# A gated linear-attention and SiLU feed-forward kernel: the state's product in two column tiles, the second product of the feed-forward without Strassen's method

## The chip, the cores and the metric

The kernel runs on one core of a Trainium2 chip. The metric is the device time of one execution in microseconds; shorter is better. Engines are named as in the profile: PE is TensorE (PEld its weight loads), DVE is VectorE, ACT is ScalarE, POOL is GpSimd, and SP is SyncE, which here only issues DMAs.

## What is computed

The inputs are `q`, `k`, `v`, `a_re`, `a_im` of shape (4, 8, 768, 48) and two weight matrices of 384 x 2048 and 2048 x 384 (the reference makes them in 64 bits; the kernel puts them together to 32 bits at the start). Cut to what matters:

```python
mag = np.sqrt(a_re * a_re + a_im * a_im)
scale = np.minimum(mag, 0.999) / (mag + 1e-06)
a = a_re * scale + 1j * a_im * scale          # per head and channel
for t in range(768):
    S = a[t][:, None] * S + outer(k[t], v[t]) # complex state, 48 x 48 per head
    y[t] = q[t] @ S.real
x = y with heads side by side                 # (3072, 384)
h = x @ w_in                                  # (3072, 2048)
out = (h * sigmoid(h)) @ w_out                # (3072, 384)
```

## The kernel before

**Tiles.** The 4 sequences of 768 steps are cut into chunks of 128 steps: 24 chunks, numbered n = 0 to 23, so that chunk n follows chunk n - 4 of the same sequence. Two chunks make a pair p = 0 to 11. The complex gates become, by logarithms and phases, a factor per step, so that a chunk's attention is plain products: `weights` (L410) makes 128 x 128 products of keys and queries for each of 8 heads, masked by DVE (L415); `output` (L431, L434) multiplies them with `v`, and adds the part from the state `S` carried from chunk n - 4; `state` (L459) makes the chunk's own part of the next state, and DVE adds and scales it (L464, L465, or L467 for a sequence's first chunk). The last chunk of each sequence makes no state, so that 20 states are made.

**The state's product.** For each of 8 heads the 128 x 96 keys (`kr`, real and imaginary part side by side) are TensorE's weights and the 128 x 48 values its moving operand; the result stands on 96 partitions of one PSUM bank. A 32-bit product is two load-and-multiply pairs on TensorE, so that the profile counts 16 for one state. `output` works in two tiles of 64 of TensorE's columns: even heads write partitions 0 to 63, odd heads 64 and up.

**Feed-forward.** A pair's 256 rows of `x` go through `hidden` (L476: eight steps of 12 matmul records of 128 x 256, each step followed by a SiLU on ACT, L245) and `result`. `result` for pairs 0 to 2 is the plain one (L518): per step two row halves times two blocks of `w_out`, 8 records of 128 x 384, in two PSUM banks. From pair 3 (`WINO = 3`, nine pairs) it is `result_of_halves` (L545): Strassen's method on halves of rows, of the inner dimension and of columns, seven products of 128 x 192 per step, 14 records. It needs four sums per step by DVE (`sums_of`, L505), combined weights made once (L493, L496), three products with zeros that open the PSUM banks (L539, per pair), and at the end of a pair an ACT copy (L552) and seven DVE additions (L556).

**What sets the order.** In the set-up (pairs 0 to 2) PE's order is written out, and a scheduler orders the other engines. From pair 3 on `step` is called under a manual schedule: all engines follow the program's order, and the strings `first` and `usual` give it token by token. In a step, `h` is a step of `hidden` and `r` one of `result`, both for the pair before; `a0A`, `a1A`, `sA`, `yA` are weights (two halves), state and output of the pair's first chunk, with B for the second; `k`, `q`, `t` rotate and turn keys and queries; `p` and `l` are the products for phases (L325) and sums (L346) of the next pair; E, D, L, F, G, th are the gates on ACT and DVE; A and X load the next inputs. ACT loads a table of functions (L240) when it changes between exponentials, arctangent and SiLU.

**Queues.** From chunk 8 on `turned` moves 12 blocks of transposed keys and queries by DMA (L401), six issued by SP and six by POOL. `output` moves six small pieces of `xT` at the end of a pair (L448), three from SP and three from POOL. SP also issues the loads, POOL the decays (`decs`, L360), ACT the stores (L529).

Of the kernel before, what the change touches and what calls it, by code (L numbers as in the profile page):

```python
# [55 lines left out]
def kernel(  # L56
# [36 lines left out]
    EARLY = 8  # L93
    RAW = 4
    WINO = 3
# [127 lines left out]
    zeros = consts.tile([1, DM], mybir.dt.bfloat16)  # L223
    nc.gpsimd.memset(zeros, 0.0)
# [30 lines left out]
    def gates_square(p, split=False):  # L255

        g = A[p]
        for x in ("s1", "s2", "mag"):
            g[x] = flat(pre.tile([C, 2, H, D], F32, tag="t3", name=f"{x}{p}", bufs=5))
        for x in ("l", "th"):  # L260
            pool = su if p == 1 else pre
            g[x] = flat(pool.tile([C, 2, H, D], F32, tag=x, name=f"{x}{p}"))
        for re, im, s1, s2, _, _, th in each(p, split):
            special(s1, re, AF.Square)
            special(s2, im, AF.Square)
            special(th, re, AF.Abs)
            nc.vector.scalar_tensor_tensor(out=s1, in0=s1, scalar=FLOOR2, in1=s2, op0=ALU.max,
                                           op1=ALU.add)
# [50 lines left out]
    def phases(n):  # L319
# [4 lines left out]
        ps = p_m.tile([C, DM], F32, tag="m", name=f"phase{n}")  # L324
# [9 lines left out]
    def trig(n):  # L334
        x = X[n]
        x["cs"] = pre.tile([C, H, 2, D], F32, tag="t3", name=f"cs{n}", bufs=5)
        special(x["cs"][:, :, 1], heads(x["turn"]), AF.Sin, scale=TWO_PI)
        special(x["cs"][:, :, 0], heads(x["turn"]), AF.Abs)
        special(x["cs"][:, :, 0], x["cs"][:, :, 0], AF.Sin, scale=-TWO_PI, bias=half_pi_b)

    def sums(n):
# [3 lines left out]
        ps = p_m.tile([C, DM], F32, tag="m", name=f"L{n}")  # L345
# [18 lines left out]
    def rotated(n, which="kq"):  # L364

        x = X[n]
        for w in which:
# [4 lines left out]
                                  bufs=2)  # L372
# [4 lines left out]
    def turned(n):  # L377
# [4 lines left out]
                                           bufs=2)  # L382
# [10 lines left out]
        else:  # L393
# [5 lines left out]
            for b in range(NB):  # L399
                for a in range(NA):  # L400
                    (nc.gpsimd if a % 2 else nc.sync).dma_start(out=to[ts(b, Q), :, a],  # L401
                                                               in_=sq[ts(a, Q), b])
# [15 lines left out]
    def output(n):  # L418
# [27 lines left out]
        for r in range(2) if i == 1 else ():  # L446
            for dc in range(ND):
                (nc.gpsimd if r and n >= EARLY else nc.sync).dma_start(  # L448
# [3 lines left out]
    def state(n):  # L452
# [5 lines left out]
        for h in range(H):  # L458
            nc.tensor.matmul(ps[:, h], lhsT=x["kr"][:, h].rearrange("p c d -> p (c d)"),  # L459
                             rhs=x["v"][:, h], start=True, stop=True)  # L460
# [10 lines left out]
    def hidden(p, jp):  # L471

        ps = p_h.tile([C, 2, T], F32, tag="h", name=f"h{p}_{jp}")
# [7 lines left out]
        if jp == 1 and late and p >= WINO:  # L481
            sums_of(p, 0)

    w2v = w2.rearrange("p (j i) (n c) -> p i n j c", i=2, n=2)

    def combined():

        for out, a, b, op in ((wc[:, 2], w2v[:, 1, 1], w2v[:, 0, 1], ALU.subtract),  # L490
                              (wc[:, 1], wc[:, 2], w2v[:, 0, 0], ALU.add),
                              (wc[:, 0], w2v[:, 1, 0], wc[:, 1], ALU.subtract)):
            nc.vector.tensor_tensor(out=out, in0=a, in1=b, op=op)  # L493

    def combined_last():
        nc.vector.tensor_tensor(out=w2v[:, 0, 1], in0=w2v[:, 0, 1], in1=w2v[:, 0, 0],  # L496
                                op=ALU.subtract)

    def sums_of(p, jp):
        g = A[p]["g", jp]  # L500
        a11, a12, a21, a22 = (g[:, i, ts(m, C)] for m in range(2) for i in range(2))
        t = late[0].tile([C, 4, C], F32, tag="gs", name=f"gs{p}_{jp}", bufs=2)
        for i, a, b, op in ((0, a21, a22, ALU.add), (1, a11, a21, ALU.subtract),
                            (2, t[:, 0], a11, ALU.subtract), (3, a12, t[:, 2], ALU.subtract)):
            nc.vector.tensor_tensor(out=t[:, i], in0=a, in1=b, op=op)  # L505
        A[p]["gs", jp] = t

    def result(p, jp):
        if late and p >= WINO:
            result_of_halves(p, jp)  # L510
            return
        if jp == 0:
            A[p]["o"] = [(late[1] if late else p_o).tile([C, 2, DM // 2], F32, tag="o",
                                                         name=f"o{p}_{m}") for m in range(2)]
        for m in range(2):
            for ji in range(2):
                j = jp * 2 + ji
                nc.tensor.matmul(A[p]["o"][m].rearrange("p n c -> p (n c)"),  # L518
                                 lhsT=A[p]["g", jp][:, ji, ts(m, C)], rhs=w2[:, j],
                                 start=(j == 0), stop=(j == NJ - 1))  # L520
        if jp == NJ // 2 - 1:
            for m in range(2):
                ot = moe.tile([C, DM], F32, tag="ot", name=f"ot{p}_{m}")
                nc.scalar.copy(out=ot, in_=A[p]["o"][m].rearrange("p n c -> p (n c)"))
                store(p, m, ot)

    def store(p, m, ot):
        b, c = place(2 * p + m)
        nc.scalar.dma_start(out=out[ts(b * NCH + c, C)], in_=ot)  # L529

    def result_of_halves(p, jp):
        if jp == 0:
            A[p]["o"] = [late[1].tile([C, 2, DM // 2], F32, tag="o", name=f"o{p}_{m}")
                         for m in range(4)]
        o = [A[p]["o"][i // 2][:, i % 2] for i in range(7)]
        g, t = A[p]["g", jp], A[p]["gs", jp]

        for x in A[p]["o"][:3] if jp == 0 else ():
            nc.tensor.matmul(x.rearrange("p n c -> p (n c)"), lhsT=zeros[:, 0:C],  # L539
                             rhs=zeros[:, 0:DM], start=True, stop=False)  # L540
        for i, a, b in ((0, g[:, 0, 0:C], w2v[:, 0, 0, jp]), (1, g[:, 1, 0:C], w2v[:, 1, 0, jp]),
                        (2, g[:, 1, C:T], wc[:, 0, jp]), (3, t[:, 0], w2v[:, 0, 1, jp]),
                        (4, t[:, 1], wc[:, 2, jp]), (5, t[:, 2], wc[:, 1, jp]),
                        (6, t[:, 3], w2v[:, 1, 1, jp])):
            nc.tensor.matmul(o[i], lhsT=a, rhs=b, start=(i == 6 and jp == 0),  # L545
                             stop=(jp == NJ // 2 - 1 and i in (1, 3, 5, 6)))
        if jp < NJ // 2 - 1:
            sums_of(p, jp + 1)
        else:
            ot = [moe.tile([C, 2, DM // 2], F32, tag="ot", name=f"ot{p}_{m}") for m in range(2)]  # L550
            c11, c12, c21, c22 = (ot[m][:, i] for m in range(2) for i in range(2))
            nc.scalar.copy(out=c11, in_=o[0])  # L552
            for to, a, b in ((c22, o[5], c11), (c21, o[4], c22), (c12, o[3], c22),
                             (c11, o[1], c11), (c12, o[6], c12), (c22, o[3], c21),
                             (c21, o[2], c21)):
                nc.vector.tensor_tensor(out=to, in0=a, in1=b, op=ALU.add)  # L556
            for m in range(2):
                store(p, m, ot[m].rearrange("p n c -> p (n c)"))
# [6 lines left out]
    def step(p, h, r, order):  # L565


        what = {"h": lambda: h(1), "r": lambda: r(1), "W": combined, "V": combined_last}
        if p < NP:
            what["E"] = lambda: (table("exp"), both(decays, p), table("silu"))  # L570
            for i, x in enumerate("AB"):
# [4 lines left out]
                for hh in range(2):  # L576
                    what[f"a{hh}{x}"] = lambda n=n, hh=hh: weights(n, hh)
                what["s" + x] = lambda n=n: state(n)
                what["y" + x] = lambda n=n: output(n)
        if p + 1 < NP:  # L580
            what["c"] = lambda: both(carry, p + 1)
            what["S"] = lambda: both(trig, p + 1)
            what["D"] = lambda: gates_square(p + 1)
            what["L"] = lambda: (table("exp"), gates_log(p + 1))
# [8 lines left out]
            what["X"] = lambda: both(load_x, p + 1)  # L593
        if p + 2 < NP:
            what["A"] = lambda: load_a(p + 2)
        for x in order.split():
# [56 lines left out]
    with tc.manual_schedule(engines={mybir.EngineType.PE}):  # L653
# [69 lines left out]
        for n in (4, 5):  # L723
# [12 lines left out]
        both(trig, 3)  # L736
        setup.close()
        late.append(fast.enter_context(tc.tile_pool(name="late", bufs=1)))
        late.append(fast.enter_context(tc.tile_pool(name="o_late", bufs=4, space=PSUM)))
        wc = late[0].tile([C, 3, NJ // 2, DM // 2], F32, tag="wc", name="wc")  # L740
    usual = ("c h E h kA qA h r tA D L kB F qB h r h tB r G h th A X a0A h a1A r sA h a0B yA r a1B "
             "r sB pA yB pB S r lA r lB")
    first = ("c h E h kA qA h r D L kB F qB h r h r tA G h th A tB X a0A h a1A r sA W h a0B yA r "
             "a1B pA sB r yB pB S r lA r lB")
    by_hand.append(True)
    with tc.manual_schedule():
        for p in range(3, NP + 1):
            order = first if p == 3 else usual
            if p == WINO + 1:
                order = "V " + order  # L750
            step(p, parts(hidden, p - 1), parts(result, p - 1), order)
# [20 lines left out]
def step_by_step(ctx, tc, q, k, v, a_re, a_im, w_in, w_out, w1, w2, out):  # L772
# [64 lines left out]


    with tc.tile_pool(name="again", bufs=2) as again:
        todo = [(w1[:, dc, ts(s, 512)], [(at, w_in[r:r + n, ts(s, 512)]) for at, r, n in  # L840
                                         rows_in(H, D, ND, dc)])
                for dc in range(ND) for s in range(w_in.shape[1] // 512)]
        todo += [(w2[:, j], [(0, w_out[ts(j, C)])]) for j in range(NJ)]
        for dst, parts in todo:
            n = dst.shape[1]
# [79 lines left out]
```

## Time and profile before

| what | value |
|---|---|
| median of 3 runs | 713.4 us (713.36 to 713.8) |
| the profiled execution's own time | 713.36 us |
| its span, first to last instruction | 711.7 us |
| mean granted TensorE clock | 0.987 of full |
| one step of the regular part (301.29 to 354.31 us) | 53.02 us |
| PE, DVE, ACT, POOL busy in that step | 53.02, 34.06, 27.57, 11.75 us |

The profile has an overall share of busy time for each engine, groups of instructions by source line, a chain of waits (the work that ended last, followed back from the end), and windows, which give each engine's busy time in a stretch. In the chain a row is: start, length, engine, tile, line, count of instructions merged. PE records overlap in time, so a single record's length is longer than its share of PE; the chain's lengths are without overlap.

### The profile page before, as it was taken

To read this page: it belongs to the slowest core of one execution; us is meant where nothing else is said; L and a number is where in the kernel's file an instruction comes from. 1 tells how busy PE (TensorE), PEld (TensorE's weight loads), DVE (VectorE), ACT (ScalarE), POOL (GpSimd) and SP (SyncE) were. 2 spreads that over 40 slices of the span, in tenths; PEclk is the share of its full clock that TensorE was granted. 3 is DMA by queue.
4 is the path that set the end of the run, shared out by engine and by line. 5 is a ranking of instruction groups with operands and counts; after the bars stand their busy time and mean duration, and the time that the engine had idled before them with its cause. 6 is when DMAs were issued, how large, how long until landed. Compare 5 with 4: busy or idle time off the path is not lost.

```text
span 711.7 us, 10959 instructions
## 1 busy us (share of the span) xinstructions
PE 661.8 (93%) x4011; PEld 567.4 (80%) x4011; DVE 429.2 (60%) x897; ACT 376.5 (53%) x603; POOL 134.1 (19%) x212
## 2 busy tenths in 40 slices
PE   0496997999999999999999999999999999999995
PEld 0275875678777689889989989889889889889895
DVE  4989858836345386476476476476476485563212
ACT  7985679458692284293293293293293293421110
POOL 2433001030000032032032032032031031050000
PEclk9998998999999999999999999999999999999998
DMA  9946347110250039038048038038038036050000
GB/s 187 234 134 161 95 134 177 45 46 4 64 96 1 18 52 158 9 65 148 17 67 150 20 62 156 19 56 157 25 49 156 29 46 113 29 78 13 30 0 28
DMA packets 160240, 55.64 MB, mean 78 GB/s; under 512 B 149272, under 2 KB 153520, under 8 KB 160176
## 3 DMA queue, kind: packets, MB, share of 16 engines
q1 hardware_dynamic: 148256, 36.85, 26.2%
q0 software_dynamic: 7424, 13.06, 11.2%
q10 hardware_dynamic: 4496, 4.92, 1.9%
q8 instruction: 34, 0.56, 0.3%
q14 instruction: 30, 0.25, 0.1%
HBM read 36.25 MB, written 4.76 MB: 58 GB/s over the span
## 4 chain that ended last, share of the span: by engine, by line
PE 88%; DVE 4%; ACT 4%; DMA 2%; issue 1%; SPq 1%; DVEq 0%; ACTq 0%
PE h L476 34%; PE o L545 23%; PE o L518 7%; PE a L410 6%; PE s L459 4%; PE y L431 3%; PE L L346 3%; PE phase L325 3%; PE y L434 2%; PE tp L389 2%; DMA raw<-in_moe_w_in_dram 1%; PE o L539 1%; ACT s L245 1%; ACT L240 1%; ACT T L392 1%
## 5 line engine op out<-in xcount | busy, mean ns | idle before, releaser
L476 PE MATMUL h<-xT,w 128*128 128x256 f32 x1152 | 262.9, 382 | 5.7 <-DMA xT<-y 5.7
L476 PEld LDWEIGHTS h<-xT,w 128*128 128x128 f32 x1152 | 217.7, 191 | 38.2 <-issue 6.2
L245 ACT ACTIVATE g<-h 128x512 f32<-128x512 f32 x96 | 55.4, 596 | 169.4 <-PE h L476 164.7
L240 ACT ACT_TABLE_LOAD x65 | 83.4, 1283 | 2.5 <-PEq L909 1.3
L415 DVE TENSOR_TENSOR w<-a,upto 128x512 f32<-128x512 f32 x48 | 33.0, 689 | 85.4 <-PE a L410 85.3
L401 POOL DMA_DIRECT2D T<-sq x96 | 61.7, 650 | 52.7 <-issue 45.6
L545 PE MATMUL o<-w,gs 128*128 128x192 f32 x288 | 70.3, 326 | 0.0
L440 ACT COPY xT<-y 128x384 f32<-128x384 f32 x24 | 11.5, 477 | 103.1 <-PE y L434 98.6
L518 PE MATMUL o<-w,g 128*128 128x384 f32 x192 | 65.1, 490 | 0.0
L360 POOL DMA_DIRECT2D decs<-ends x48 | 30.4, 640 | 182.4 <-DMA ends<-eq 170.4
L505 DVE TENSOR_TENSOR gs<-g 128x128 f32<-128x128 f32 x144 | 35.1, 285 | 44.1 <-PE o L545 23.9
L545 PE MATMUL o<-w,g 128*128 128x192 f32 x288 | 60.5, 332 | 0.0
L545 PE MATMUL o<-wc,gs 128*128 128x192 f32 x288 | 58.6, 326 | 0.0
L545 PEld LDWEIGHTS o<-w,g 128*128 128x128 f32 x288 | 47.9, 190 | 9.3 <-issue 4.5
L518 PEld LDWEIGHTS o<-w,g 128*128 128x128 f32 x192 | 36.3, 191 | 23.7 <-issue 1.5
L410 PEld LDWEIGHTS a<-T 96*128 96x128 f32 x384 | 49.2, 192 | 4.2 <-DVE w L415 1.0
L410 PE MATMUL a<-T 96*128 96x128 f32 x384 | 50.4, 276 | 1.0 <-DVE w L415 0.8
L545 PEld LDWEIGHTS o<-w,gs 128*128 128x128 f32 x288 | 50.8, 190 | 0.0
L545 PEld LDWEIGHTS o<-wc,gs 128*128 128x128 f32 x288 | 48.8, 190 | 0.0
L448 POOL DMA_DIRECT2D xT<-y x24 | 11.9, 502 | 182.3 <-ACT y L444 182.3
L325 PE MATMUL phase<-th,upto 128*128 128x384 f32 x48 | 23.0, 579 | 21.0 <-DVE th L304 18.4
L431 PE MATMUL y<-w,v 128*64 128x128 f32 (+1 forms) x384 | 39.6, 281 | 0.0
(90 smaller groups left out, 957.3 us busy)
## 6 DMA issues: line engine op xcount, KB each, us to landing
raw<-in_moe_w_out_dram SPq DMA_DIRECT2D x16, 384.0 KB
T<-sq SPq DMA_DIRECT2D x96, 64.0 KB
T<-sq POOLq DMA_DIRECT2D x96, 64.0 KB, 4.2
raw<-in_moe_w_in_dram SPq DMA_DIRECT2D x24, 192.0 KB
out_dram<-ot ACTq DMA_DIRECT2D x24, 192.0 KB
re<-in_a_re_dram SPq DMA_DIRECT2D x18, 192.0 KB
k<-in_k_dram SPq DMA_DIRECT2D x18, 192.0 KB
q<-in_q_dram SPq DMA_DIRECT2D x18, 192.0 KB
```

The source lines that it names most:

```text
L240: chain(nc.scalar.preload_act_table_set({"exp": "natural_log_exp_and_others", "trig": "trig_and_small", "silu": "silu_and_others"}[of]))
L245: chain(nc.scalar.activation(out=out, in_=in_, func=func, **kw))
L325: nc.tensor.matmul(ps, lhsT=upto, rhs=th, start=True, stop=True)
L360: nc.gpsimd.dma_start(out=decs[a * D:(a + 1) * D, n], in_=ends[n].rearrange("(h d) -> d h", d=D))
L401: (nc.gpsimd if a % 2 else nc.sync).dma_start(out=to[ts(b, Q), :, a], in_=sq[ts(a, Q), b])
L410: nc.tensor.matmul(ps[:, h], lhsT=x["kT"][:, hh * HH + h], rhs=x["qT"][:, hh * HH + h], start=True, stop=True)
L415: nc.vector.tensor_tensor(out=x["w", hh], in0=ps, in1=upto.unsqueeze(1).to_broadcast([C, HH, C]), op=ALU.mult)
L431: nc.tensor.matmul(to, lhsT=v_[:, cols], rhs=x["w", h // HH][:, h % HH], start=True, stop=not carried)
L476: nc.tensor.matmul(ps[:, ji], lhsT=w1[:, dc, ts(jp * 2 + ji, C)], rhs=A[p]["xT"][:, dc], start=(dc == 0), stop=(dc == ND - 1))
L505: nc.vector.tensor_tensor(out=t[:, i], in0=a, in1=b, op=op)
L518: nc.tensor.matmul(A[p]["o"][m].rearrange("p n c -> p (n c)"), lhsT=A[p]["g", jp][:, ji, ts(m, C)], rhs=w2[:, j], start=(j == 0), stop=(j ...
L545: nc.tensor.matmul(o[i], lhsT=a, rhs=b, start=(i == 6 and jp == 0), stop=(jp == NJ // 2 - 1 and i in (1, 3, 5, 6)))
```

## The change

It does several things at once.

1. `state` makes each head's product as two: 64 of the key's columns to partitions 0 to 63, then 32 to partitions 64 to 95. There are 16 products for each state in place of 8, 32 records in place of 16, in the order 64, 32, 64, 32 and so on.
2. Strassen's method is gone with all that belongs to it: `result` is the plain one for all pairs. `sums_of`, `combined`, the products with zeros and the seven additions fall away; ACT copies two 128 x 384 results per pair.
3. PSUM is shared out anew: two banks for results in place of four, one more for `hidden` (each third step), one for phases and sums.
4. The order of a step is another. E, L and F follow each other with one exponential table between them; D (squares of the gates) is done for two pairs ahead, at the end of a step, so that the first stands ahead of step 3; both halves of `weights` follow each other, then phases, state and output (`aA pA sA yA`).
5. All 12 blocks of L401 and all six pieces of L448 are issued by SP.
6. More buffers: gates' `l` and `th` two, `t3` six, `kr` three, `T` three.

The way for extreme inputs (`step_by_step`), which this input does not take, reloads the weights only if they are in 64 bits; that part is left out below.

```diff
@@ state @@
         ps = p_m.tile([D2, H, D], F32, tag="m", name=f"s{n}")
         for h in range(H):
-            nc.tensor.matmul(ps[:, h], lhsT=x["kr"][:, h].rearrange("p c d -> p (c d)"),
-                             rhs=x["v"][:, h], start=True, stop=True)
+
+            for m in (ds(0, 64), ds(64, D2 - 64)):
+                nc.tensor.matmul(ps[m, h], lhsT=x["kr"][:, h].rearrange("p c d -> p (c d)")[:, m],
+                                 rhs=x["v"][:, h], start=True, stop=True)
@@ phases, sums @@
-        ps = p_m.tile([C, DM], F32, tag="m", name=f"phase{n}")
+        ps = (late[3] if late else p_m).tile([C, DM], F32, tag="m", name=f"phase{n}")
...
-        ps = p_m.tile([C, DM], F32, tag="m", name=f"L{n}")
+        ps = (late[3] if late else p_m).tile([C, DM], F32, tag="m", name=f"L{n}")
@@ gates_square @@
-            g[x] = flat(pre.tile([C, 2, H, D], F32, tag="t3", name=f"{x}{p}", bufs=5))
+            g[x] = flat(pre.tile([C, 2, H, D], F32, tag="t3", name=f"{x}{p}", bufs=6))
         for x in ("l", "th"):
-            pool = su if p == 1 else pre
-            g[x] = flat(pool.tile([C, 2, H, D], F32, tag=x, name=f"{x}{p}"))
+            g[x] = flat(pre.tile([C, 2, H, D], F32, tag=x, name=f"{x}{p}", bufs=LB))
@@ turned @@
-                                           bufs=2)
+                                           bufs=3 if late else 2)
...
-                    (nc.gpsimd if a % 2 else nc.sync).dma_start(out=to[ts(b, Q), :, a],
-                                                               in_=sq[ts(a, Q), b])
+                    nc.sync.dma_start(out=to[ts(b, Q), :, a], in_=sq[ts(a, Q), b])
@@ output @@
-                (nc.gpsimd if r and n >= EARLY else nc.sync).dma_start(
+                nc.sync.dma_start(
@@ hidden @@
-        ps = p_h.tile([C, 2, T], F32, tag="h", name=f"h{p}_{jp}")
+        pool = late[2] if late and jp % 3 == 2 else p_h
+        ps = pool.tile([C, 2, T], F32, tag="h", name=f"h{p}_{jp}")
...
-        if jp == 1 and late and p >= WINO:
-            sums_of(p, 0)
@@ result @@
-        if late and p >= WINO:
-            result_of_halves(p, jp)
-            return
...
             for m in range(2):
+                b, c = place(2 * p + m)
                 ot = moe.tile([C, DM], F32, tag="ot", name=f"ot{p}_{m}")
-                nc.scalar.copy(out=ot, in_=A[p]["o"][m].rearrange("p n c -> p (n c)"))
-                store(p, m, ot)
...
+                nc.scalar.copy(out=ot, in_=A[p]["o"][m])
+                nc.scalar.dma_start(out=out[ts(b * NCH + c, C)], in_=ot)
@@ step @@
-            what["E"] = lambda: (table("exp"), both(decays, p), table("silu"))
+            what["E"] = lambda: (table("exp"), both(decays, p))
...
-                for hh in range(2):
-                    what[f"a{hh}{x}"] = lambda n=n, hh=hh: weights(n, hh)
+                what["a" + x] = lambda n=n: (weights(n, 0), weights(n, 1))
...
-            what["D"] = lambda: gates_square(p + 1)
-            what["L"] = lambda: (table("exp"), gates_log(p + 1))
+            what["L"] = lambda: gates_log(p + 1)
...
+            what["D"] = lambda: gates_square(p + 2)
@@ the steps @@
+        gates_square(4)
         setup.close()
         late.append(fast.enter_context(tc.tile_pool(name="late", bufs=1)))
-        late.append(fast.enter_context(tc.tile_pool(name="o_late", bufs=4, space=PSUM)))
-        wc = late[0].tile([C, 3, NJ // 2, DM // 2], F32, tag="wc", name="wc")
-    usual = ("c h E h kA qA h r tA D L kB F qB h r h tB r G h th A X a0A h a1A r sA h a0B yA r a1B "
-             "r sB pA yB pB S r lA r lB")
-    first = ("c h E h kA qA h r D L kB F qB h r h r tA G h th A tB X a0A h a1A r sA W h a0B yA r "
-             "a1B pA sB r yB pB S r lA r lB")
+        late.append(fast.enter_context(tc.tile_pool(name="o_late", bufs=2, space=PSUM)))
+        late.append(fast.enter_context(tc.tile_pool(name="h_late", bufs=1, space=PSUM)))
+        late.append(fast.enter_context(tc.tile_pool(name="m_late", bufs=1, space=PSUM)))
+    usual = ("c h h E kA qA L F h kB h tA G r qB r h tB r th h A X r h r aA pA sA yA h pB aB S r lA "
+             "sB yB r lB D r")
+    first = ("c h h E kA qA L F h kB h G r qB r h th r tA h A tB X r h r aA pA sA yA h pB aB S r lA "
+             "sB yB r lB D r")
```

## The prediction

> **What bounds the kernel now.** I read the shares of busy time first, then the windows, then the chain of waits in one regular step.
>
> ```profile
> PE 661.8 (93%) x4011; PEld 567.4 (80%) x4011; DVE 429.2 (60%) x897; ACT 376.5 (53%) x603; POOL 134.1 (19%) x212
> ...
> PE 88%; DVE 4%; ACT 4%; DMA 2%; issue 1%; SPq 1%; DVEq 0%; ACTq 0%
> ```
>
> The first row is of busy time, the second of the chain that ended last: PE is the bound by both. The windows say how strictly. Columns: length, then PE, PEld, DVE, ACT, POOL busy with their counts, granted clock, DMA share, GB/s.
>
> ```profile
> 248.27:301.29 53.02, 53.02 (x348) 47.95 (x348) 34.28 (x71) 27.57 (x40) 11.68 (x19) 1.00 0.44 74
> 301.29:354.31 53.02, 53.02 (x348) 47.95 (x348) 34.06 (x75) 27.57 (x40) 11.75 (x19) 1.00 0.44 78
> ```
>
> In the regular steps PE never rests and the clock is full; DVE and ACT rest a third of the time or more. So what leaves DVE (the sums for Strassen's method) is worth nothing, and what is added to PE is paid in full. The chain through a step (start, length, engine, tile, line, records) gives the prices:
>
> ```profile
> 301.29 7.77 PE h L476 x36
> 309.06 0.59 PE o L539 x3
> 309.64 2.47 PE o L545 x14
> 312.12 2.59 PE h L476 x12
> 314.71 2.28 PE o L545 x14
> ...
> 331.15 1.32 PE s L459 x16
> 332.47 2.66 PE h L476 x12
> 335.13 0.89 PE a L410 x8
> 336.02 0.38 PE y L431 x4
> 336.40 0.22 PE y L434 x4
> 336.62 0.26 PE y L431 x4
> 336.88 0.22 PE y L434 x4
> ...
> 337.99 2.47 PE o L545 x14
> ```
>
> Three things are to be seen. A group of Strassen's takes 2.28 us, or 2.47 when the records before it used another tiling (L539 after its one-row weights, L434 after its tiles of 64 columns). The first records of `y` after full-width `a` take 0.38 where later ones take 0.22. And a state is 16 records in 1.32 us, 82.5 ns each.
>
> **Strassen's method goes: +14.6 us.** The plain step of `result` stands in the same trace, for pairs 0 to 2, as
>
> ```profile
> 199.79 2.58 PE o L518 x8
> ```
>
> A pair costs 0.59 + 2.47 + 7 x 2.28 = 19.0 us now and 8 x 2.58 = 20.6 us then: +1.62 us, on PE, for nine pairs (L539 has 27 records, three a pair): +14.6 us. The DVE work that goes (L505, L493, L496, L556) lay beside PE but at the end.
>
> **The end: -1.8 us.** After the last product DVE adds, and nothing covers it:
>
> ```profile
> 694.83 8.79 PE o L545 x54
> 703.62 0.04 DVEq L556
> ...
> 705.54 0.36 DVE ot L556
> ```
>
> From 703.62 to 705.90 is 2.28 us. The plain way has one ACT copy of 128 x 384 there, 0.48 us by L524's row; the copy of the first row half lies under the second half's products (4 x 0.32 us). The stores after it are the same.
>
> **The order of step 3: -1 us.** Around 208 to 216 us PE rests 2.4 us in all, between transposes (L389), since ACT's copies (L392) stand behind a table load, an arctangent and another load. In the new `first` the transposes come after these loads. I take -1, bounds -3 and +2.
>
> **Moves I cost at nothing, with their cover.** *Blocks of L401, all on SP.* SP issues one in 0.656 us (median), so 12 need 7.9 us. The first chunk's blocks are ready some 15.5 us into the step: the first decayed keys come at 8.1 (two `h` of 2.59, a SiLU of 0.6, a table load of 1.28, two exponentials of 0.52), and then DVE has kA and qA (0.55 + 0.96 each), one sum of L (0.9), kB (1.5) and two transposes (0.96 each), 7.3 us. So they are issued by 23.4 and, with the 4.2 us to landing that POOL's show, are there by 28; `aA` starts on PE at about 31 (7 `h` at 2.59 and 5 `r` at 2.58). The second's land at about 36, and `aB` starts at about 41. The loads A (4 at about 1.1 us) and X (6 at about 0.8) queue behind them until about 41, ahead of L448, which is due at 50. Cover gone would cost what is late, 3 us of slack at the least. *Six pieces of L448 on SP.* In the early part all six already go by SP: `y` ends at 54.50 and `h` starts at 60.22, 5.7 us, with one landing of 3.03 us among weight loads. The new order has `r lB D r` between, 2.58 + 0.65 + 2.58 and 0.19 for leaving `y`'s tiles: 6.0 us. It fits, barely; each issue (0.59) too late would cost 0.6 us a step. *SiLU waits for E, L and F.* From the third `h` on, ACT has to finish two table loads (1.28 each), four exponentials (0.52), five passes of L and two of F (0.8 to 0.9): about 16 us into the step, and SiLU of the third group at 16.7. Its first user, the third `r`, is at 18.2. *D earlier, buffers, PSUM:* ACT has 25 us of rest in a step, and no rotation that I followed comes round before its reader is done. `aA pA sA yA` puts phases and state between weights and `y`, over 1.9 us, where DVE needs 0.69 for each mask.
>
> So without the state's product: 713.4 (this execution's own time, 713.36, which is the median of the runs; span 711.7) + 14.6 - 1.8 - 1.0 = **725.2 us**.
>
> **The state's product.** It is 320 records in 20 states (L459), all on the chain. Each head becomes a tile of 64 columns and one of 32. The trace has no two tiles of different width side by side, so I bound it.
>
> *If a change of width makes TensorE wait.* Every change of tiling in the trace costs: full width to 64 columns 0.38 - 0.22 = 0.16 us, 64 to full 2.47 - 2.28 = 0.19 (0.84 against 0.65 us where phases follow). A part of that is the new weights' load, which nothing hides: 82.5 ns for 96 columns is 0.86 ns a column, so 0.055 for 64 and 0.11 for 128. The wait itself is then 0.105 and 0.08, say 0.093. A 48-row product streams in 0.04 us (216 ns for 256 rows of L476). A head is then, for 64 columns, 0.093 + 0.055 + 0.055 (the second load is longer than the first product) + 0.04 = 0.243; for 32 columns 0.093 + 0.028 + 2 x 0.04 = 0.201; together 0.444, eight heads 3.55 us in place of 1.32: +2.23 a state, **+44.6 us** for 20. Bounds: if the loads hide in the waits, a head is 0.36, 2.9 us a state, +31; if each of 16 changes costs the whole 0.19 on top of the present 1.32, 4.36 a state, +61.
>
> *If it does not.* In `output` two tiles of equal width run side by side: 4 records in 0.22 us, 55 ns each, though each streams 128 rows, 107 ns. Were 64 and 32 such a couple, the 64-column tile would set the pace, two loads of 0.055 a head: 0.88 us a state, -0.44, -8.8 us for 20. With 55 ns a record as a floor, 32 records are 1.76 us: +0.44, +8.8 us.
>
> I take the first, since all three kinds of change in the trace (128 to 64 columns, 64 to 128, one-row weights to full rows) cost the same 0.08 to 0.1 us of waiting, and the free case in the trace is only of equal widths.
>
> The Trainium skill, "TensorEngine Tiling (Array Packing)", section "Key Properties", speaks against this change: it says that changing the tiling mode, not just the tile, drains the TensorE, and it lists 64 and 32 columns as different modes. The rows agree for changes from and to full width; no row here shows 64 to 32. The same page's "Theoretical Speedup" promises up to twice for a small dimension, which would be the sum of the second case.
>
> **Forecast: 725.2 + 44.6 = 769.8 us**, its own range 755 to 786.
>
> **Rivals.**
>
> *1. No wait between unequal tiles.* For it: `y`'s odd and even tiles overlap at no price, and 64 and 32 share no column. Against it: no change of width in the trace was free. Time 725.2 - 8.8 = **716.4** by the loads, up to 725.2 + 8.8 = 734.0 with 55 ns a record.
>
> *2. Not slower: the loads hide too.* If loads of the two tiles and of successive heads ran ahead under the products, a head would take its streaming alone, 2 x 0.04 us: 0.64 us a state, -0.68, -13.6 for 20: **711.6**. It decides from a head below 0.1 us on: then 20 states save the 11.8 us that the rest costs. Against it: in full-width `s` a load of 0.08 shows whole although each product is 0.04, so loads do not run ahead by more than one.
>
> *3. The wait, and SP late as well.* The forecast's mechanism with one or two issues of L448 late in eight steps, 8 x 0.6 to 8 x 1.2: 5 to 10 us more, **775 to 780**. Its cover of 0.3 us is thin, but the 3.03 us landing that I compared with was under weight loads.
>
> **How the numbers follow.** The wait, with SP in time, 0.62; the wait with SP late 0.08; no wait, paced by loads or records, 0.26 (two thirds near 716, one third up to 734); loads hidden too, 0.04. The predicted time is the first's, 769.8. The two cases with the wait hold 0.70, of which some 0.03 lies above 784 or so; to leave out no more than 0.2 the range has to reach down over rival 1: 715 to 785. 0.2%, 1.4 us, is about what a measurement of this kernel can tell from no change. Faster by over that (below 712.0) is most of rival 2 and the lowest edge of rival 1: 0.04. Within it (712.0 to 714.8): the rest of rival 2 and the fastest loads of rival 1, 0.04. Slower: 0.92.
>
> **What would show it.** In the chain of the changed kernel `s` should have 32 records a state in about 3.5 us (rival 1: 0.9 or 1.8; rival 2: 0.64), and a regular step should take 53.02 + 1.62 + 2 x 2.23 = 59.1 us (rival 1: 53.8 to 55.5). `result` should show 2.58 us for 8 records in all pairs and no L505. PE should still be busy through each step; a rest of PE before `h` released by the DMA of `xT` would be rival 3, one before `r` released by ACT would show the cover of SiLU gone. What would make me wrong at the root: that a change of width costs only where the columns of the two tiles overlap, which all changes in the trace do.

## The result, and the profile after

The changed kernel takes 770.3 us (median of 4 runs, 769.7 to 776.5) against 713.6 for the kernel before (four runs, 713.4 to 713.8): a ratio of 1.0815, 95% interval 1.0759 to 1.087. The profiled execution took 770.71 us; its span is 769.0. The forecast was 769.8.

On the page of the changed kernel, the shares of busy time and the chain's shares by engine:

```profile
PE 720.5 (94%) x3872; PEld 538.8 (70%) x3872; DVE 333.8 (43%) x542; ACT 363.4 (47%) x597; POOL 60.2 (8%) x91
...
PE 86%; ACT 5%; DMA 3%; DVE 3%; SPq 2%; issue 1%; ACTq 0%
```

PE is the bound as before. It is busy 59 us longer with fewer records, and its weight loads are busy less: time has gone into PE that is neither more products nor more loads. DVE's 95 us less were worth nothing but at the end (below). Two regular steps by the windows (length, then PE, PEld, DVE, ACT, POOL busy with counts, granted clock, DMA share, GB/s):

```profile
323.46:382.46 59.00, 59.00 (x329) 44.14 (x329) 24.30 (x35) 25.66 (x39) 2.51 (x4) 1.00 0.38 70
382.46:443.04 60.58, 60.58 (x329) 45.66 (x329) 24.30 (x35) 25.66 (x39) 2.51 (x4) 0.97 0.38 68
```

The step grew from 53.02 to 59.00 us (59.1 were forecast), PE without a rest. The second has the same records and 1.58 us more, at a clock of 0.97: that was not foreseen, and comes back below. The chain through such a step, changed kernel:

```profile
333.82 5.16 PE o L487 x16
338.98 2.59 PE h L475 x12
341.57 2.58 PE o L487 x8
...
354.49 1.79 PE a L406 x16
356.28 0.65 PE phase L322 x2
356.92 3.58 PE s L457 x32
360.50 0.38 PE y L427 x4
```

A state is 3.58 us where it was 1.32 (3.55 were forecast); a group of `result` is 2.58, as the plain one was before. Nothing else in this step is dearer.

### The profile page after: what moved, and what is told of

Its sections match the earlier page's. It is cut to its first block, busy times and chain, and to the rows that moved or that the text cites. A ratio compares the mean times of both kernels' runs of the same rounds, so it can differ in the third digit from the quotient of the medians.

```text
span 769.0 us, 10128 instructions
## 1 busy us (share of the span) xinstructions
PE 720.5 (94%) x3872; PEld 538.8 (70%) x3872; DVE 333.8 (43%) x542; ACT 363.4 (47%) x597; POOL 60.2 (8%) x91
## 4 chain that ended last, share of the span: by engine, by line
PE 86%; ACT 5%; DMA 3%; DVE 3%; SPq 2%; issue 1%; ACTq 0%
PE h L475 31%; PE o L487 30%; PE s L457 9%; PE a L406 5%; PE y L427 4%; PE y L430 3%; PE phase L322 2%; PE L L343 2%; PE tp L386 2%; DMA raw<-in_moe_w_in_dram 1%; ACT s L243 1%; ACT L238 1%; ACT mag L243 1%; DMA q<-in_q_dram 1%; SPq L135 1%
## 5 line engine op out<-in xcount | busy, mean ns | idle before, releaser
L487 PE MATMUL o<-w,g 128*128 128x384 f32 x768 | 261.1, 488 | 0.0
L487 PEld LDWEIGHTS o<-w,g 128*128 128x128 f32 x768 | 144.1, 190 | 89.0 <-issue 2.2
L457 PE MATMUL s<-v,kr 128*32 128x48 f32 (+1 forms) x640 | 73.5, 230 | 0.4 <-DVE w L411 0.2
L457 PEld LDWEIGHTS s<-v,kr 128*32 128x32 f32 (+1 forms) x640 | 52.8, 122 | 26.9 <-issue 7.6
L366 DVE TENSOR_TENSOR L<-k,L 128x384 f32<-128x384 f32 x24 | 13.3, 554 | 82.5 <-ACT L L243 82.5
L346 DVE TENSOR_SCALAR L<-L 128x384 f32<-128x384 f32 x24 | 13.4, 557 | 55.6 <-PE L L343 55.3
L430 PE MATMUL y<-T,S 96*64 96x128 f32 x320 | 36.7, 291 | 0.0
L324 DVE TENSOR_SCALAR turn<-phase 128x384 f32<-128x384 f32 x24 | 13.4, 557 | 44.7 <-PE phase L322 44.6
L243 ACT ACTIVATE mag<-mag 128x768 f32<-128x768 f32 (+1 forms) x39 | 30.6, 790 | 0.4
L243 ACT ACTIVATE s<-s 128x768 f32<-128x768 f32 (+1 forms) x39 | 30.5, 786 | 0.4
```

The costliest lines, as they stand in the source:

```text
L243: chain(nc.scalar.activation(out=out, in_=in_, func=func, **kw))
L430: nc.tensor.matmul(to, lhsT=x["S"].rearrange("p h d -> p (h d)")[:, cols], rhs=x["qT"][:, h], start=False, stop=True)
L457: nc.tensor.matmul(ps[m, h], lhsT=x["kr"][:, h].rearrange("p c d -> p (c d)")[:, m], rhs=x["v"][:, h], start=True, stop=True)
L487: nc.tensor.matmul(A[p]["o"][m], lhsT=A[p]["g", jp][:, ji, ts(m, C)], rhs=w2[:, j], start=(j == 0), stop=(j == NJ - 1))
```

## The experiments

My theory: TensorE waits whenever the next product has another tile width, and then shows that product's load. Rival A: each record of a narrow tile costs 0.112 us (3.58 / 32), whatever stands beside it. Rival B: tiles of 32 columns are slow in themselves. Rival C: part of the loss belongs to the new order or to SP's queue. Each kernel was timed in three rounds, beside the kernel before on the same chip (713.0 us for the first four, 711.3 for the next, 710.9 for the last). The first four are equal width, full width, the other order and three tiles; the last is the one with the states parted. Medians of different groups come from different chips, so that between groups the ratios count, and steps of the profiles. In all diffs lines that do not matter are left out.

### Two tiles of equal width

```diff
-            for m in (ds(0, 64), ds(64, D2 - 64)):
-                nc.tensor.matmul(ps[m, h], lhsT=x["kr"][:, h].rearrange("p c d -> p (c d)")[:, m],
-                                 rhs=x["v"][:, h], start=True, stop=True)
+            for at in (0, 64):
+                nc.tensor.matmul(full[at:at + 64, h], lhsT=x["kf"][:, ds(h * D2 + at, 64)],
+                                 rhs=x["v"][:, h], start=True, stop=True)
```

`full` is the PSUM bank on all 128 partitions, `kf` the keys of all heads with 32 zero columns behind the last, set by POOL.

> The changed kernel with the state's product in two tiles of equal width: 64 columns at 0 and 64 at 64 (the second takes 32 columns of the next head along, whose results nobody reads). Theory (a change of tile width makes TensorE wait 0.093 us and shows the next load): no change of width within a state, so the 64-column tile paces it with two loads of 0.055 us a head: 0.88 us a state in place of 3.58, a regular step of 53.6 us in place of 59.0, time 770.3 - 20 x 2.70 = 716.3 us. Rival A (each record of a narrow tile costs 0.112 us, whatever its neighbour): 32 records still, 3.58 us a state, 770 us. Rival B (a tile of 32 columns is slow in itself): as the theory here.

Measured: 715.1 us, a ratio to the kernel before of 1.0031 (1.0018 to 1.0044). The chain of this kernel:

```profile
330.59 0.65 PE phase L322 x2
331.24 1.07 PE s L461 x32
332.31 0.27 PE y L431 x4
332.57 0.22 PE y L434 x4
```

The same number of records as in the changed kernel, 1.07 us in place of 3.58 (0.88 were expected); `y` behind it starts in 0.27 in place of 0.38, since it finds its tile width already set. Rival A is dead: 55 us have gone by a change of the second tile's width alone. Neither a product's place in the array (columns 0 and 64 still take turns) nor the shared PSUM bank is the cause.

### Full width again

```diff
-            for m in (ds(0, 64), ds(64, D2 - 64)):
-                nc.tensor.matmul(ps[m, h], lhsT=x["kr"][:, h].rearrange("p c d -> p (c d)")[:, m],
-                                 rhs=x["v"][:, h], start=True, stop=True)
+            nc.tensor.matmul(ps[:, h], lhsT=x["kr"][:, h].rearrange("p c d -> p (c d)"),
+                             rhs=x["v"][:, h], start=True, stop=True)
```

> The changed kernel with the state's product at full width again, 16 records of 96 columns; all else of the change stays. Theory: the state alone carries 20 x (3.58 - 1.32) = 45.2 us, so 725.1 us, a regular step of 54.5 us, and what is left against the kernel before is Strassen's method (+14.6), the end (-1.8) and the third step. Rival C (part of the loss is SP's or ACT's, from blocks and pieces all on SP or from the new order): more than 727 us, with rests of PE before h or r.

Measured: 722.1 us (718.9 to 723.7), ratio 1.0141 (1.0109 to 1.0172). So everything in the change but the state's product costs 9 us, and the state's product 48: 20 x 2.26 = 45.2 by its length, and the rest is of the size of the pieces of low clock (below). A regular step by the windows of this kernel:

```profile
351.91:406.39 54.48, 54.48 (x298) 41.92 (x297) 24.29 (x35) 25.63 (x39) 2.50 (x4) 1.00 0.41 75
```

54.48 us, PE without a rest: 1.46 more than with Strassen's method. Rival C is dead in the regular steps: the order, the 12 blocks and the six pieces on SP cost nothing there.

### The same records in another order

```diff
-        for h in range(H):
-
-            for m in (ds(0, 64), ds(64, D2 - 64)):
+        for m in (ds(0, 64), ds(64, D2 - 64)):
+            for h in range(H):
```

> The same 32 records a state as in the changed kernel, in another order: the 64-column tiles of all 8 heads, then the 32-column tiles of all 8. Theory: one change of width inside a state in place of 15: 16 records at 0.055 us and 16 at 0.04, two waits of 0.093: about 1.75 us a state, time 770.3 - 20 x 1.83 = 733.7 us. Rival A (cost per narrow record): 770 us. Rival B (the 32-column tile is slow in itself, some 0.1 us a record): about 2.7 us a state, 753 us.

Measured: 730.8 us, ratio 1.026 (1.0232 to 1.0288). The chain of this kernel:

```profile
335.56 0.65 PE phase L322 x2
336.21 1.86 PE s L456 x32
338.07 0.38 PE y L427 x4
```

The very same 32 products take 1.86 us when the width changes twice, and 3.58 when it changes 16 times: (3.58 - 1.86) / 14 = 0.123 us for a change. That would fit the wait of 0.093 with a load of 0.028 to 0.055 shown now and then, but no run takes the two apart: only their sum is shown. Both theories of a price per record fail here, B by 22 us.

### Three tiles of 32 columns

```diff
-            for m in (ds(0, 64), ds(64, D2 - 64)):
+            for m in (ds(0, 32), ds(32, 32), ds(64, 32)):
```

> The changed kernel with the state's product in three tiles of 32 columns at 0, 32 and 64: 48 records a state, one width. Theory: no change of width inside a state; by streaming alone (two products of 0.04 us a head in each of three tiles at once) 0.64 us a state, 711.5 us; if records cannot follow each other faster than some 25 ns, 1.2 us, 722.7 us. Rival A (0.112 us for each narrow record): 5.4 us a state, 806 us. Rival B (32 columns slow in themselves, 0.1 us a record): 4.8 us a state, 795 us.

Measured: 713.6 us, ratio 1.0018 (1.0003 to 1.0034). The chain of this kernel:

```profile
329.60 0.65 PE phase L322 x2
330.25 0.81 PE s L457 x48
331.06 0.38 PE y L427 x4
```

48 records in 0.81 us, 17 ns each. Streaming alone is 0.64 us (8 heads of 2 x 0.04), and the 0.17 left fit one change of width: three tiles run at once, loads included (48 loads at the estimated 0.028 us would be 1.3 us one after the other). It decides against B, and it is what my second rival had asked for, loads that hide: in tiles of one width they do.

### The split alone, in the kernel before

The edit of `state` as in the changed kernel (first part of the diff), nothing else; Strassen's method and the old order stay.

> The kernel before, with Strassen's method and its own order, and only the state's product split into 64 and 32 columns. Theory (wait at every change of width): 20 states at 3.58 in place of 1.32 us, +45.2, and in the regular steps the state now stands beside full-width products, which shows their load, 14 x 0.12 = +1.7 us: 759.9 us; if the split also pulls TensorE's granted clock down for a window now and then, as in the changed kernel's profile, up to 766. Rival C (part of the loss belongs to the new order and queues): below 757 us.

Measured: 762.8 us (759.6, 759.7, 766.0 and 766.2), ratio 1.0711 (1.0658 to 1.0765). The split costs about as much alone (51.5 us; 48.3 in the two faster runs) as in company (48). The four times fall in two groups some 6.4 us apart, with mean clocks of 0.989 and 0.968; the profile is of the slowest, with four pieces at half clock in its regular steps.

### Three tiles alone, in the kernel before

```diff
-            nc.tensor.matmul(ps[:, h], lhsT=x["kr"][:, h].rearrange("p c d -> p (c d)"),
-                             rhs=x["v"][:, h], start=True, stop=True)
+            for m in (ds(0, 32), ds(32, 32), ds(64, 32)):
+                nc.tensor.matmul(ps[m, h], lhsT=x["kr"][:, h].rearrange("p c d -> p (c d)")[:, m],
+                                 rhs=x["v"][:, h], start=True, stop=True)
```

> The kernel before with only the state's product in three tiles of 32 columns. Theory: 0.81 us a state, as in the changed kernel's version of it, in place of 1.32: -10.2 us for 20, +1.7 us for 14 states that now stand between full-width products: 704.5 us, faster than both kernels. Rival D (the kernel before has no room for it, because DVE or another engine sets the regular step of 53.02 us): 711 to 713 us, no change.

Measured: 705.7 us, ratio 0.9922 (0.9892 to 0.9951): 0.8% faster than the kernel before. A regular step by its windows:

```profile
349.99:402.25 52.26, 52.26 (x412) 46.61 (x412) 34.06 (x75) 27.57 (x40) 11.73 (x19) 1.00 0.45 79
```

0.76 us less than the 53.02 before, by two states of 0.51 less each and some 0.13 a state for leaving narrow tiles once more. PE alone set that step; rival D is dead.

### The state beside the output

As the last, with another order: a state directly ahead of an output.

```diff
-    usual = ("... X a0A h a1A r sA h a0B yA r a1B r sB pA yB pB S r lA r lB")
+    usual = ("... X a0A h a1A r h sA yA a0B r a1B r pA sB yB pB S r lA r lB")
```

> As the kernel before with three tiles of 32 columns, and the order of the regular steps changed so that a state stands directly ahead of an output, with which it shares narrow tiles (h sA yA a0B in place of sA h a0B yA; pA sB yB in place of sB pA yB). Theory: the 14 x 0.12 us for leaving narrow tiles once more go: 702.8 us, 1.7 below the version without the new order. Rival D: 711 to 713. A new wait (PSUM banks of the weights not yet masked when the state wants one) would show as a rest of PE before s, up to 0.7 us a state, 712.

Measured: 707.8 us, ratio 0.994 (0.992 to 0.9961): no gain on the 705.7 of the version before it, and the expectation of 702.8 was wrong. The chain of this kernel, at the pair's second chunk:

```profile
341.16 0.66 PE phase L325 x2
341.82 0.02 issue
341.84 0.57 DVE turn L327
342.41 0.02 issue
342.43 0.57 DVE turn L329
343.00 0.04 issue
343.05 0.45 PE y L431 x4
```

`y` needs the PSUM bank that the phases hold until DVE has read them twice. Before, `pA` stood there with `sB` ahead of it and `a1B` had freed the other bank; now 0.8 us of state is all that covers 1.2 us of DVE, and PE rests 0.4 us. The step is 52.37 us against 52.26. A piece at half clock in the third step costs this profile another 1.6 us (a half of `a` takes 2.08 in place of 1.16, the `h` behind it 3.29 in place of 2.59), so the 2.1 us between the medians need not all be the order's. I named a wait for a bank, and put it at the wrong bank.

### The split after the set-up only

```diff
-            for m in (ds(0, 64), ds(64, D2 - 64)):
+            for m in (ds(0, 64), ds(64, D2 - 64)) if n >= 6 else (ds(0, D2),):
```

> The changed kernel with the state's product at full width for the 6 states of the set-up, and split in 64 and 32 for the 14 after it. Theory: 14 x 2.26 = +31.6 us on the full-width version's 722.1: 753.7 us; each window of 3.4 us at half clock that the waits bring on costs 1.6 more, two or three of them: 755 to 759. If the clock in the first 100 us (0.86 in the changed kernel, 0.91 to 0.97 in the others) is pulled down by the split, it is back at 0.91 or more here; if it is chance, it may be 0.86 again.

Measured: 758.7 us (757.6 to 761.3), ratio 1.0663 (1.0631 to 1.0696). From the start of step 3 to PE's end the profile takes 567.8 us (186.68 to 754.51), the full-width version's 529.8 (182.52 to 712.27): 38.1 more, of which the waits of 14 states explain 14 x 2.26 = 31.6. The rest is the clock: four pieces at half clock, some 1.6 us each. Two stretches of this kernel by the windows, a state and the `y` behind it:

```profile
345.72:349.30 3.58, 3.58 (x34) 2.62 (x36) 1.15 (x3) 0.00 (x0) 0.00 (x0) 1.00 1.03 203
349.30:352.81 3.51, 3.51 (x33) 3.15 (x33) 1.11 (x2) 0.00 (x0) 0.00 (x0) 0.52 1.09 214
```

`y` takes 3.5 us at half clock in place of 2.0. It follows a state of 3.58 us that was mostly waiting, though the profile counts PE as busy in it. The question of the first 100 us stays open: their clock is 0.97 here, but 0.91 in the full-width version and 0.90 in the next kernel, which do not split there either, and 0.86 in the changed kernel.

### The states parted

The last kernel, with each state in two parts of four heads and a full-width group between them.

```diff
-    def state(n):
+    def state(n, part=None):
...
-        for h in range(H):
+        for h in range(H) if part is None else range(part * HH, part * HH + HH):
...
-    usual = ("... X r h r aA pA sA yA h pB aB S r lA "
+    usual = ("... X r h r aA pA uA h sA yA pB aB S uB r lA "
              "sB yB r lB D r")
```

`uA` and `uB` are the first parts, `sA` and `sB` the second; `first` is changed alike.

> As the kernel that splits only the 14 states after the set-up, with each of these states parted: heads 0 to 3, a full-width group of 2.6 us (a step of hidden or of result), heads 4 to 7. The waits are as many; what changes is that no stretch of them is longer than 1.8 us in place of 3.58. Theory of the clock (a stretch of waits as long as the 3.4 us pieces of half clock brings such a piece on): no half-clock piece in the regular steps, where the unparted kernel had four in its profile; time 753.7 + 14 x 0.2 for leaving narrow tiles once more = 756.5 us at a mean granted clock of 0.985 or more, less spread between runs. If the pieces are chance or come from the total share of waits, three or four of them stay, with 1.6 us each: 761 to 763.

Measured: 756.7 us (756.0 to 758.7), ratio 1.0643 (1.0613 to 1.0673). Two of its steps by the windows:

```profile
309.15:368.67 59.52, 59.47 (x329) 44.14 (x329) 24.30 (x35) 25.66 (x39) 2.50 (x4) 1.00 0.38 69
368.67:428.18 59.51, 59.46 (x329) 44.13 (x329) 24.29 (x35) 25.66 (x39) 2.50 (x4) 1.00 0.38 69
```

Every regular step has this length, and none has a piece at half clock, where three steps of the unparted kernel had one and took 60.6 us. A parted step is 0.5 us longer than one of 59.00. This is one profile of each. The median is 2.0 us lower, but it was taken on another chip, and the intervals of the two ratios overlap: the steps show the effect, the whole time does not yet.

## Why the prediction was right

The sum against the profiled executions, cut where step 4 starts (`h` of three or four groups at 248.27 and 264.46) and where PE ends (703.62 and 764.09):

| stretch | forecast | measured |
|---|---|---|
| to the start of step 4: 8 states, the third step | 8 x 2.23 - 1.0 = +16.8 | +16.2 |
| step 4 to PE's end: Strassen's, 12 states | 14.6 + 12 x 2.23 = +41.4 | +44.3 |
| after PE's end | -1.8 | -3.1 |

**The state's product** was the step that decided, and it was right in its mechanism and its size: 3.58 us against 3.55, so 20 x 2.26 = 45.2 us and not 44.6. How much of a change is wait and how much load was not tested. The price came from `y`'s neighbours in the trace of before, with the wait taken apart from the load. What I named as the root of a possible error, that a change of width might cost only where two tiles overlap, is refuted: 64 and 32 share no column, and a change costs 0.123 us, not far from the 0.16 and 0.19 of before. The Trainium skill, "TensorEngine Tiling (Array Packing)", section "Key Properties", was the right rule to weigh: a change of the mode drains, a change of the tile does not. The runs agree with both halves (3.58 against 1.07 us), which the trace of before could not show.

**Strassen's method** was 14.0 us in the full-width version's profile (step 4 to PE's end, 469.3 against 455.4 us), not 14.6. A step is 1.46 and not 1.62 dearer, since the order spares some: the phases stood behind a state and an output (0.71 and 0.84 us) and take 0.65 each now.

**The end** was mis-sized: -3.1 and not -1.8. The additions were counted rightly (2.28 us against 0.48), but "the stores after it are the same" was wrong: from the last copy to the end it is 4.4 us, and was 5.8 from the last addition. The first half's store is now issued at 763.33, ahead of PE's end, where both were issued from 705.28 on, behind it.

**The third step** fell further than forecast, within its bounds. PE's rests between the transposes are 0.7 us in the changed kernel and were 2.4. From its first `h` to that of step 4 the step takes 62.7 us in the kernel before and 60.5 in the full-width version: -2.2 in place of -1.0. In the changed kernel it takes 65.0, 4.5 more for two split states.

**What I cost at nothing** cost nothing: no PE rest in a regular step, not before `h` for the pieces of `xT` from SP, not before `r` for SiLU. The third rival did not come.

**What I left out** is the clock: two pieces at half clock in the regular steps of the changed kernel's profile and one ahead of them, some 1.6 us each. Without them the profiled execution would have been 766. Against the forecast that is -0.6 for Strassen's method, -1.3 for the end, -1.2 for the third step, +0.6 for the states, +4.7 for the clock, and some -1.2 in the set-up that no run explains. So the forecast's 0.5 us from the median is luck: errors of up to 5 us cancel. The cause it named is shown.

## What to carry to other kernels

Splitting a narrow product into column tiles paid here when all tiles had one width: 96 columns as 3 x 32 took 0.81 us in place of 1.32, less some 0.13 where full-width products followed; as 64 + 32 in turn they took 3.58. Price a change of tile width by the first product behind such a change in any trace (here 0.12 to 0.19 us), and count the changes, not the products. An engine that the profile shows as busy may be waiting inside: compare the time of a group with its records' streaming.

## What the runs showed of the hardware that I had not expected

TensorE's granted clock falls to half for a piece of 3.41 us behind some stretches of such waits of 3.58 us, and behind none of 1.8 us. The four pieces of the kernel split after the set-up, by the windows:

```profile
243.62:247.03 3.41, 3.41 (x34) 3.30 (x32) 1.11 (x2) 0.00 (x0) 0.00 (x0) 0.50 0.02 5
349.43:352.84 3.41, 3.41 (x33) 3.05 (x30) 1.01 (x2) 0.00 (x0) 0.00 (x0) 0.50 1.09 216
468.90:472.31 3.41, 3.41 (x32) 3.17 (x32) 1.11 (x2) 0.00 (x0) 0.00 (x0) 0.50 1.15 226
588.37:591.78 3.41, 3.41 (x34) 3.31 (x33) 1.11 (x2) 0.00 (x0) 0.00 (x0) 0.50 1.11 217
```

The Trainium skill, "TensorE: Matmul & The Clock Gate", section "What's actually happening", gives a free-running window of 3413 ns over which activity is judged. The traces agree: the starts above lie 31.0, 35.0 and 35.0 such windows apart (105.81, 119.47 and 119.47 us). They also tell which states are hit. In the three profiles with unparted states of 64 and 32 columns in turn, 42 such states stand after the set-up, and 10 have a piece of half clock behind them. These are the ones that hold a whole window of this grid but for at most 0.23 us; in the other 32 every window sticks out by 0.28 us or more. A parted state of 1.8 us cannot hold one. And three tiles of equal width take a record every 17 ns, with loads of all three running at once.
